# Eight short rows of unread matmuls behind the k steps of one phase of a tuned DFT and expert-mixture kernel

## The chip, the cores and the metric

The kernel runs on one core of a Trainium2 chip. The metric is the device time of one execution in microseconds (us). The engines are TensorE (PE, with its weight loads as PEld), VectorE (DVE), ScalarE (ACT), GpSimd (POOL) and SyncE (SP), which issues most DMAs.

## The reference

The output mixes two branches of one input x of 2048 tokens by 512 features, with a gate per token. Branch A is a two-sided DFT, of which the real part is kept. Branch B is a sum over 8 experts with softmax gates.

```python
a = einsum("bsd,ed->bse", x, dft_hid_re);  b = einsum("bsd,ed->bse", x, dft_hid_im)
A = einsum("ts,bse->bte", dft_seq_re, a) - einsum("ts,bse->bte", dft_seq_im, b)
B = sum_e softmax(xf @ w_gate)_e * (silu(xf @ w1[e]) @ w2[e])
out = g * A + (1 - g) * B          # g = sigmoid((x * gate_w).sum(-1))
```

## The kernel before

All large products are made of fp32r matmuls in three parts. A matrix is split into a high and a low piece, and the helper `mm` (lines 348 to 353) issues high x high (L349), high x low (L352) and low x high (L353) into one accumulator in PSUM. An accumulator is one bank, 128 partitions x 512 fp32; the pool `psp` has all 8 banks. A matmul takes 128 x 128 weights and 128 rows x 512 columns of the moving operand. Matmuls without a split, in plain fp32, occur at two places: ten in the warm-up (`warm`, L603, 128 x 128 columns) and the logits (L387), where each group of four puts its 32 columns of weights on a column tile of the array of its own.

The sequence DFT comes first. It has eight phases, by half of the output, by group of columns and by kind (X or Y). Each phase loops over NK = 8 values of k; for one k, a phase X issues the products 1, 2 and 5, each for two halves n, which is 18 matmuls into six banks, and a phase Y issues 6, 3, 7 and 4 into eight. The change concerns the phase (pr, c, ph) = (1, 1, "X"), the last phase X. Its predecessor is (1, 0, "Y") and its successor (1, 1, "Y"). For each k, `plan_right` loads a piece of the DFT matrix (SP), forms sums and splits it (DVE, ACT, once POOL); `plan_out_x` and `plan_out_y` read the finished banks (ACT and DVE) and store them. Behind the DFT come the second product of branch A and the experts, whose order is found by the planner `Plan`.

What sets the order: every operation is put on a list with a planned time (`ev`), the list is sorted, and the functions are called in that order. Compute instructions that are pinned (`pin`) keep this order on their engine; DMAs are not pinned, and the framework places them on SP's queue. It also assigns the banks of the pool and inserts the waits.

Of the kernel before, what the change touches and what calls it, by code (L numbers as in the profile page):

```python
# [8 lines left out]
F32 = mybir.dt.float32  # L9
# [7 lines left out]
P = 128  # L17
# [3 lines left out]
GT = 512  # L21
# [275 lines left out]
def fnet_moe_kernel(ctx: ExitStack, tc: tile.TileContext, x, xT, cT, wd, w1d, w2d, wg, out):  # L297


    nc = tc.nc  # L300
# [7 lines left out]
    psp = ctx.enter_context(tc.tile_pool(name="psp", bufs=8, space=PSUM))  # L308
    dram = ctx.enter_context(tc.tile_pool(name="dram", bufs=1, space=DRAM))

    def f32(ap_):
        return ap_.bitcast(F32)

    def sl(i):
        return slice(i * P, (i + 1) * P)
# [16 lines left out]
    def ev(t, fn, *args):  # L332

        evs.append((base[0] + t, len(evs), fn, args))

    def pin(ins):
        tc.keep_in_program_order(ins)
# [10 lines left out]
    def mm(ps, lh, ll, rh, rl, start, stop, first):  # L348
        ins = nc.tensor.matmul(ps, lh, rh, start=start, stop=False, skip_group_check=True)  # L349
        if first:  # L350
            pin(ins)
        nc.tensor.matmul(ps, lh, rl, start=False, stop=False, skip_group_check=True)  # L352
        nc.tensor.matmul(ps, ll, rh, start=False, stop=stop, skip_group_check=True)  # L353
# [21 lines left out]
    def plan_logits(T, dt):  # L375

        v = {}

        def load(d, a):
            v[d, a] = stage.tile([P, 2, GT], F32, tag="stage", name=f"xr{d}_{a}")  # L380
            nc.sync.dma_start(v[d, a], xT[d, :, 2 * a * GT:2 * (a + 1) * GT].rearrange("p (g t) -> p g t", g=2))

        def dots(d):
            if d == 0:
                v["p"] = psp.tile([P, GT], F32, tag="p", name="lt")
            for g in range(NG):
                ins = nc.tensor.matmul(v["p"][g * SQ:(g + 1) * SQ, :], wgs[:, d, :], v[d, g // 2][:, g % 2, :],  # L387
                                       start=d == 0, stop=d == ND - 1, skip_group_check=True)
                if g == 0:
                    pin(ins)  # L390

        def turn():
            pin(nc.vector.transpose(lg, v["p"]))

        ev(T - 12, lambda: nc.sync.dma_start(wgs[:, :, :E1], wg))
        for d in range(ND):
            t = T + dt * (1, 3, 5, 6)[d] + 2.6
            for a in range(2):
                ev(t - 9 + a, load, d, a)
            ev(t, dots, d)  # L400
        ev(t + 2.4, turn)
# [34 lines left out]
    xl, five, xraw = {}, {}, {}  # L436
# [8 lines left out]
    def plan_left_x(k, s, s5=None):  # L445

        v = {}
        s5 = s if s5 is None else s5

        def load(a, b):  # L450
            if a == 0:
                xraw[k] = xp.tile([P, 4, 256], F32, tag="x", name=f"xr{k}")
            nc.sync.dma_start(xraw[k][:, a:b, :], x[k][:, a:b, :])

        def s1():
            v["q"] = tmp.tile([P, 256], F32, tag="c", name=f"xq{k}_0")
            vt(v["q"], xraw[k][:, 2, :], xraw[k][:, 3, :], add)

        def hi():
            if k % 2 == 0:  # L460
                five[0] = xp.tile([P, 2, 2, 256], F32R, tag="x", name=f"xl5_{k}")
            v["w"] = five[0]
            act(v["w"][:, 0, k % 2, :], v["q"])
            xl[5, k] = (v["w"], k % 2)

        if s5 == s:
            ev(s - 14.5, load, 0, 4)
        else:
            ev(s - (14.5 if k else 31.5), load, 0, 2)
            ev(s5 - 14.5, load, 2, 4)  # L470
        left_pair(s - 4.7, s - 4.0, 1, 2, k, lambda: xraw[k][:, 0:2, :])
        ev(s5 - 3.3, s1)
        ev(s5 - 2.4, hi)
        ev(s5 - (0.9 if k == 1 else 0.5),
           lambda: vt(v["w"][:, 1, k % 2, :], v["q"], f32(v["w"][:, 0, k % 2, :]), sub))

    def plan_left_y(k, s, dt=None):

        v = {}

        def s3():
            v["q"] = tmp.tile([P, 2, 256], F32, tag="c", name=f"xq{k}_1")
            vt(v["q"][:, 0, :], xraw[k][:, 0, :], xraw[k][:, 2, :], sub)

        t = [s + dt * n for n in range(5)] if dt else [s, s + 0.5, s + 1.0, s + 2.0, s + 3.2]
        ev(t[0], s3)
        ev(t[1], lambda: vt(v["q"][:, 1, :], xraw[k][:, 3, :], v["q"][:, 0, :], sub))
        ev(t[2], lambda: vt(xraw[k][:, 1, :], xraw[k][:, 1, :], v["q"][:, 1, :], sub))
        left_pair(t[3] - 1.0, t[3], 7, 6, k, lambda: v["q"])
        left_pair(t[4] - 1.5, t[4], 3, 4, k, lambda: xraw[k][:, 1:4:2, :])  # L490
# [64 lines left out]
    def plan_right_0(k, s, s5, r):  # L555

        v = {}

        def load():
            v["a"] = stage.tile([P, 2, GT], F32, tag="stage", name=f"ca0{k}")  # L560
            if k:
                nc.sync.dma_start(v["a"], cT[0, 0, k][:, 0:2, :])
                return
            for j, queue in enumerate((nc.scalar, nc.sync)):
                queue.dma_start(v["a"][:, j, :], cT[0, 0, k][:, j, :])

        def load_d():
            v["d"] = tmp.tile([P, GT], F32, tag="c", name=f"cd0{k}")
            nc.sync.dma_start(v["d"], cT[0, 0, k][:, 2, :])

        def at(t_hi, t_lo, pool, tag, m, src):
            split_at(t_hi, t_lo, lambda: pool.tile([P, 2, GT], F32R, tag=tag, name=f"c0{k}_{m}"), src, vt,
                     lambda w: r.__setitem__(m, (w[:, 0, :], w[:, 1, :])))

        ev(s - (14.4 if k else 31), load)
        ev(s5 - 14.4, load_d)
        at(s - 4.0, s - 3.2, cp, "w", 1, lambda: v["a"][:, 0, :])
        at(s - 3.3, s - 2.6, cp, "w", 2, lambda: v["a"][:, 1, :])
        ev(s5 - 2.6, lambda: vt(v["d"], v["d"], v["a"][:, 0, :], sub))
        at(s5 - 1.8, s5 - (0.8 if k else 0.3), gp, "g", 5, lambda: v["d"])  # L580
# [24 lines left out]
    def dft(pr, c, k, ms, r, ps):  # L605
        for m in ms:
            w, j = xl[m, k]
            for n in range(2):
                if k == 0:
                    ps[m, n] = psp.tile([P, GT], F32, tag="p", name=f"u{pr}{c}_{m}{n}")  # L610
                mm(ps[m, n], w[:, 0, j, sl(n)], w[:, 1, j, sl(n)], *r[m], k == 0, k == NK - 1, True)

    def u_out(t, pr, c, i, j, n):
        nc.sync.dma_start(ud[c, 2 * pr + j, 2 * i + n], t[:, n, :])

# [100 lines left out]
    for pr, c, ph in phases:  # L716
        first = before is None
        dt = TY if ph == "Y" else TX0 if first else TXL if (pr, c) == (1, 0) else TX
        ps = {}
        for k in range(NK):  # L720
            s, r = T + k * dt, {}
            if first:
                if k < 2:
                    s, s5 = T + 2.72 * k, T + 5.44 + 1.36 * k
                    plan_left_x(k, s, s5)
                    plan_right_0(k, s, s5, r)
                    ev(s, dft_0, k, (1, 2), r, ps)
                    ev(s5, dft_0, k, (5,), r, ps)
                    continue
                plan_left_x(k, s)  # L730
                plan_right(pr, c, ph, k, s - 14, s - 2.9, r, lo=s - 3.4 if k == 2 else None)
            else:
                t = s - (6.8 if ph == "X" else 8.3)
                if before == "Y" and k == 1:
                    plan_right(pr, c, ph, k, t - 7, T - 4.0, r, pt, T - 2.1)
                else:
                    if before == "Y" and k == 2:
                        t = T + 3.4
                    plan_right(pr, c, ph, k, t - 7, t, r)
            ev(s, dft, pr, c, k, (1, 2, 5) if ph == "X" else (6, 3, 7, 4), r, ps)  # L740
        at = lambda k, o=0.0: T + k * dt + o
        if (pr, c, ph) == (0, 1, "X"):
            for k in range(NK - 3):
                plan_left_y(k, T + 6.2 * k + 0.4, 1.3)
        if (pr, c, ph) == (0, 0, "Y"):
            for k in range(NK - 3, NK):
                plan_left_y(k, T + 0.8 + (k - NK + 3) * 2.2 * TY, TY / 2)
        if (pr, c, ph) == (1, 0, "X"):
            plan_logits(T, dt)
        if (pr, c, ph) == (1, 0, "Y"):  # L750
            ev(at(2), softmax)
            ev(at(2, 4), softmax_end)
        if (pr, c, ph) == (1, 1, "X"):
            ev(at(2, 3.5), gate_rows)
            for n in range(4):
                plan_wd(n // 2, 2 * (n % 2), at(4 + n))
        if (pr, c, ph) == (1, 1, "Y"):
            for n in range(4):
                plan_uv0(n // 2, 2 * (n % 2), at(3 + n, 1))
        T += NK * dt  # L760
        if ph == "X":
            plan_out_x(pr, c, T, ps)
        else:
            plan_out_y(pr, c, T, ps, 14 if (pr, c) == (0, 0) else 7.5)
        before = ph
# [162 lines left out]
    for m in XORDER[:NX]:  # L928
# [4 lines left out]
        k = XORDER.index(m)  # L933
# [625 lines left out]
```

## Time and profile before

| | |
|---|---|
| median of 2 runs | 2020.7 us (2019.18 and 2022.22) |
| the profiled execution | 2019.07 us, its span 2017.3 us |
| PE busy | 2005.3 us, 99% of the span, 8836 matmul records |
| DVE, ACT, POOL busy | 82%, 51%, 42% |
| DMA | 475.19 MB, 236 GB/s on average |
| granted TensorE clock | 1.000 on average |

The span runs from the first to the last instruction. Busy shares are of the span. A matmul's record holds its whole passage through the engine, so neighbours overlap; the distance between two starts tells what one of them costs. An fp32 matmul is two records.

### The profile page before, as it was taken

Reading aid. Unit: us, or ns where it says so; the run is one execution under the profiler, and the core shown is the slowest. Engines: PE = TensorE matmul, PEld = TensorE weight load, DVE = VectorE, ACT = ScalarE, POOL = GpSimd, SP = SyncE. Lnnn points to the kernel's source line nnn. Section 1 sums busy time; section 2 is a strip of 40 time slices with the busy share of each in tenths; the row PEclk is TensorE's granted clock in tenths of the full one; section 3 lists DMA queues with packets and bytes.
Section 4 is the critical chain, followed back from the end, with each engine's and each line's share of the span. In section 5 each row is a group of like instructions: output and inputs, shape, how many; then the busy total and the mean of one; then the engine's idle time right before and its main releaser. Section 6 shows DMA issues by size and latency. Waiting matters only on the chain. (4 is left out here: it accounts for less than half of the span.)

```text
span 2017.3 us, 26775 instructions
## 1 busy us (share of the span) xinstructions
PE 2005.3 (99%) x8836; PEld 1651.1 (82%) x8836; DVE 1649.3 (82%) x1910; ACT 1020.9 (51%) x1427; POOL 848.9 (42%) x825
## 2 busy tenths in 40 slices
PE   9999999999999999999999999999999999999998
PEld 7887888888888888888878888888888888888887
DVE  8996996887878887887788787687778887899885
ACT  6543453455555555555555555544444444445442
POOL 0000000288889888889898820000002221233330
PEclk9999999999999999999999999999999999999999
DMA  8686686545565546454645599899889988999991
GB/s 316 215 269 215 237 306 218 187 149 179 173 202 172 188 159 213 165 194 164 222 156 176 177 307 377 296 338 288 266 264 289 289 269 257 285 282 323 315 284 42
DMA packets 204595, 475.19 MB, mean 236 GB/s; under 512 B 23172, under 2 KB 37892, under 8 KB 204456
## 3 DMA queue, kind: packets, MB, share of 16 engines
q1 hardware_dynamic: 191640, 450.15, 64.6%
q0 software_dynamic: 12672, 23.07, 6.8%
q8 instruction: 69, 1.13, 0.2%
q14 instruction: 70, 0.57, 0.1%
q10 hardware_dynamic: 144, 0.26, 0.1%
HBM read 366.36 MB, written 107.03 MB: 235 GB/s over the span
## 5 line engine op out<-in xcount | busy, mean ns | idle before, releaser
L1169 ACT ACTIVATE psp<-psp 128x512 f32<-128x512 f32 x280 | 160.3, 582 | 207.9 <-DVE psp L1153 141.3
L1153 DVE TENSOR_TENSOR psp<-psp,tc 128x512 f32<-128x512 f32 x79 | 55.3, 699 | 34.5 <-PE psp L353 28.1
L1068 POOL TENSOR_TENSOR tc<-ras 128x256 f32<-128x256 f32 x27 | 19.9, 738 | 137.2 <-DMA ras<-w_dram 135.9
L1231 ACT ACTIVATE tc<-psp 128x512 f32<-128x512 f32 x88 | 52.5, 597 | 43.6 <-PE psp L353 35.3
L1398 POOL DMA_DIRECT2D xfx1n<-w_dram x11 | 9.8, 978 | 128.1 <-DVE xf211n L1455 94.9
L1231 ACT ACTIVATE tg<-psp 128x512 f32<-128x512 f32 x67 | 40.0, 597 | 35.5 <-PE psp L353 26.3
L1153 DVE TENSOR_TENSOR psp<-psp,tg 128x512 f32<-128x512 f32 x52 | 36.3, 699 | 22.2 <-PE psp L353 16.8
L340 POOL TENSOR_TENSOR c73011l<-cb,c73011h 128x1024 fp32r<-128x1024 f32 x1 | 2.4, 2400 | 116.9 <-DMA ca<-cT_dram 116.9
L1083 POOL TENSOR_TENSOR wfs1nn<-tc,wfs1nn 128x512 fp32r<-128x512 f32 x32 | 41.9, 1311 | 15.6 <-ACT wfs1nn L1081 15.4
L1179 DVE TENSOR_TENSOR tc<-psp,tc 128x512 f32<-128x512 f32 x62 | 42.5, 685 | 5.3 <-ACT psp L1169 4.5
L1068 POOL TENSOR_TENSOR tc<-tc,ras 128x256 f32<-128x256 f32 x54 | 43.1, 798 | 4.2 <-DVE xfx13n L968 1.8
L1083 POOL TENSOR_TENSOR wfs3n<-tc,wfs3n 128x512 fp32r<-128x512 f32 x29 | 38.4, 1323 | 11.1 <-ACT wfs3n L1081 10.8
L1083 POOL TENSOR_TENSOR wfs2n<-tc,wfs2n 128x512 fp32r<-128x512 f32 x29 | 39.0, 1345 | 8.9 <-ACT wfs2n L1081 8.9
L1231 ACT ACTIVATE tw<-psp 128x512 f32<-128x512 f32 x41 | 24.5, 597 | 30.0 <-PE psp L353 24.6
L1083 POOL TENSOR_TENSOR wfs0n<-tc,wfs0n 128x512 fp32r<-128x512 f32 x26 | 35.3, 1356 | 7.8 <-ACT wfs0n L1081 7.6
L1153 DVE TENSOR_TENSOR psp<-psp,tw 128x512 f32<-128x512 f32 x37 | 25.9, 699 | 15.5 <-PE psp L353 13.5
L346 ACT ACTIVATE c<-cd 128x512 fp32r<-128x512 f32 x32 | 20.2, 631 | 33.0 <-DVE cd L343 32.6
L349 PE MATMUL psp<-xfx,wfs0n 128*128 128x512 f32 x94 | 36.7, 390 | 0.1
L353 PE MATMUL psp<-xfx,wfs0n 128*128 128x512 f32 x94 | 36.6, 389 | 0.0
L1083 POOL TENSOR_TENSOR wfs0n<-tg,wfs0n 128x512 fp32r<-128x512 f32 x24 | 32.2, 1340 | 7.7 <-ACT wfs0n L1081 7.7
L340 POOL TENSOR_TENSOR c12111l<-ca,c12111h 128x1024 fp32r<-128x1024 f32 x1 | 2.6, 2602 | 77.1 <-PE u L353 77.1
L1083 POOL TENSOR_TENSOR wfs3n<-tg,wfs3n 128x512 fp32r<-128x512 f32 x24 | 32.9, 1370 | 3.2 <-ACT wfs3n L1081 3.1
(3459 smaller groups left out, 7933.3 us busy)
## 6 DMA issues: line engine op xcount, KB each, us to landing
hd<-tc SPq DMA_DIRECT2D x161, 256.0 KB, 2.3
ca<-cT_dram SPq DMA_DIRECT2D x63, 512.0 KB, 5.6
hd<-tg SPq DMA_DIRECT2D x108, 256.0 KB, 2.4
hd<-tw SPq DMA_DIRECT2D x75, 256.0 KB, 2.4
cb<-cT_dram SPq DMA_DIRECT2D x32, 512.0 KB, 5.7
ras<-w_dram SPq DMA_DIRECT2D x29, 512.0 KB, 4.3
xfx12n<-hd SPq DMA_DIRECT2D x27, 512.0 KB, 5.8
ras1n<-hd SPq DMA_DIRECT2D x26, 512.0 KB, 4.8
```

The source lines that it names most:

```text
L340: pin(nc.gpsimd.tensor_tensor(*a))
L346: pin(nc.scalar.activation(dst, src, f, **kw))
L349: ins = nc.tensor.matmul(ps, lh, rh, start=start, stop=False, skip_group_check=True)
L353: nc.tensor.matmul(ps, ll, rh, start=False, stop=stop, skip_group_check=True)
L1068: pin(ins.tensor_tensor(low(b, j), src(x), src(y), o))
L1083: lambda: pin(nc.gpsimd.tensor_tensor(r(w)[:, 1, :], f(b), f(w)[:, 0, :], sub)), [oh] + deps, [b, w],
L1153: q = op("DVE", V, due, lambda: pin(nc.vector.tensor_tensor(f(dst), f(a[0]), f(b_[0]), o)), [a[1], b_[1]] + list(deps), [dst, a[0], b_[0]] ...
L1169: os = op("ACT", A, due, lambda: pin(nc.scalar.activation(f(dst), f(src_), AF.Silu, scale=sign)), [o0], [dst, src_])
L1179: oh = op("DVE", V, due + 1.2, lambda: pin(nc.vector.tensor_tensor(f(hb), f(dst), f(gb), OP.mult)), [os, og], [hb, dst, gb], lock=dst.ring ...
L1231: o = op("ACT", AP_, after(x), lambda: pin(nc.scalar.activation(f(b), f(bank[x[0]]), AF.Copy)), [prod[x]], [b, bank[x[0]]])
L1398: return op("POOL", 0.9, due, lambda: pin(nc.gpsimd.dma_start(f(src_)[:, j, :], block(key), accum_op=add, max_dma_last_dim=4096)), deps, [ ...
```

## The change

A new function `spare` is called behind the matmuls of each k in the phase (1, 1, "X"). It issues a row of matmuls on the operands of that k (the weight tiles w0 and w1 of product 1 and the moving piece m) into two banks of its own, `unread0` and `unread1`, which nothing reads. The output is computed as before. The rows differ from the plain stream in one thing each:

- k = 0: six matmuls of 256 columns, two weight tiles in turn
- k = 1: six with the same weight tile
- k = 2: six on the upper 64 rows of the array
- k = 3: six with 64 columns of weights
- k = 4: twelve, on the lower-numbered and the higher-numbered 64 rows in turn, on two banks
- k = 5: three in fp32 instead of fp32r
- k = 6: six that each open the sum anew
- k = 7: six on two banks in turn

```diff
+    unread = {}
+
+    def spare(k, r):
+
+        if k == 0:
+            for n in range(2):
+                unread[n] = psp.tile([P, GT], F32, tag="p", name=f"unread{n}")
+        a, b = unread[0], unread[1]
+        w, j = xl[1, k]
+        w0, w1 = w[:, 0, j, sl(0)], w[:, 0, j, sl(1)]
+        m = r[1][0]
+        half = slice(0, GT // 2)
+        low, high = slice(0, P // 2), slice(P // 2, P)
+        many = {
+            0: [(a[:, half], (w0, w1)[i % 2], m[:, half], False) for i in range(6)],
+            1: [(a, w0, m, False) for i in range(6)],
+            2: [(a, (w0, w1)[i % 2][low], m[low], False) for i in range(6)],
+            3: [(a[low], (w0, w1)[i % 2][:, low], m, False) for i in range(6)],
+            4: [((a, b)[i % 2], w0[(low, high)[i % 2]], m[(low, high)[i % 2]], False) for i in range(12)],
+            5: [(a, f32((w0, w1)[i % 2]), f32(m), False) for i in range(3)],
+            6: [(a, (w0, w1)[i % 2], m, True) for i in range(6)],
+            7: [((a, b)[i % 2], (w0, w1)[i % 2], m, False) for i in range(6)],
+        }[k]
+        for i, (ps, lhs, rhs, st_) in enumerate(many):
+            ins = nc.tensor.matmul(ps, lhs, rhs, start=st_ or i < (2 if k in (4, 7) else 1), stop=True,
+                                   skip_group_check=True)
+            if i == 0:
+                pin(ins)
...
             ev(s, dft, pr, c, k, (1, 2, 5) if ph == "X" else (6, 3, 7, 4), r, ps)
+            if (pr, c, ph) == (1, 1, "X"):
+                ev(s, spare, k, r)
```

On PE the rows stand between the plain matmuls of one k and those of the next. The first of them, in the piece of the difference below (u are the plain accumulators, xl the weights, c the moving pieces):

```order
 L352 MATMUL u_51_2132<-c_2064,xl_0_176 128x512
 L353 MATMUL u_51_2132<-c_2064,xl_0_176 128x512
+L637 MATMUL unread_2136<-c12110h,xl_12_115 128x256 x6
 L349 MATMUL u_10_2112<-c12111h,xl_12_130 128x512
 L352 MATMUL u_10_2112<-c12111l,xl_12_130 128x512
```

Six matmuls are new and the rows around them are the same. It is so at all eight places; on DVE, ACT and POOL no instruction moves.

On SP the queue changes at one place, near the end of the phase. Before (ca and cb are pieces of the DFT matrix for the next phase, tc<-xT_dram pieces of x for the experts, ud<-c finished results):

```order
L535 DMA ca_2332<-cT_dram 128x1024
L535 DMA cb_2334<-cT_dram 128x1024
L432 DMA tc_2792<-gTd 128x512
L535 DMA ca_2372<-cT_dram 128x1024
L535 DMA cb_2374<-cT_dram 128x1024
L903 DMA tc_2826<-xT_dram 128x512
L535 DMA ca_2454<-cT_dram 128x1024
```

And with the change:

```order
L535 DMA ca_2373<-cT_dram 128x1024
L535 DMA cb_2375<-cT_dram 128x1024
L432 DMA tc_2845<-gTd 128x512
L934 DMA tc_2879<-xT_dram 128x512
L934 DMA tc_2881<-xT_dram 128x512
L934 DMA tc_2900<-xT_dram 128x512
L535 DMA ca_2419<-cT_dram 128x1024
L535 DMA cb_2421<-cT_dram 128x1024
L934 DMA tc_2904<-xT_dram 128x512
```

Three loads of x now stand ahead of the next pair ca and cb; the fourth, which stood further back as well, comes right behind it.

## Rows read from the trace of the kernel before

**Rows 1.** The page: busy time of the engines, the granted clock in 40 slices of the span, and the chain that ended last, by engine and by line.
```profile
PE 2005.3 (99%) x8836; PEld 1651.1 (82%) x8836; DVE 1649.3 (82%) x1910; ACT 1020.9 (51%) x1427; POOL 848.9 (42%) x825
PEclk9999999999999999999999999999999999999999
PE 49%; DVE 0%; ACT 0%; issue 0%
PE psp L349 16%; PE psp L353 16%; PE psp L352 16%; DVE xfx9n L1360 0%; DVE xf31nn L1360 0%; ACT tw L1231 0%
```
**Rows 2.** Busy time by stretch: from:to, length, then PE, PEld, DVE, ACT and POOL busy (number of records), granted clock, DMA share, GB/s. The logits begin in the first stretch, the second is the changed phase, the third the phase behind it, and the last holds a stop of PE.
```profile
169.00:175.00 6.00, 6.00 (x30) 4.02 (x29) 5.52 (x7) 2.21 (x3) 0.00 (x0) 1.00 0.92 296
245.00:277.40 32.40, 32.40 (x144) 26.84 (x143) 30.14 (x42) 17.33 (x24) 0.00 (x0) 1.00 0.82 284
277.40:322.00 44.60, 44.60 (x198) 36.94 (x197) 39.98 (x48) 20.58 (x21) 0.00 (x0) 1.00 0.66 220
411.00:417.00 6.00, 4.97 (x22) 3.79 (x21) 4.61 (x5) 5.41 (x10) 3.56 (x4) 1.00 0.38 95
```
**Rows 3.** Instructions in order of time within the phase, PE and then its weight loads: start us, duration us, engine, line, operation, out<-in, array tile, shape.
```profile
270.62 0.39 PE L349 MATMUL u<-c12116h,xl 128*128 128x512 f32 x1
270.85 0.39 PE L352 MATMUL u<-c12116l,xl 128*128 128x512 f32 x1
...
272.66 0.39 PE L349 MATMUL u<-c,xl 128*128 128x512 f32 x1
...
270.62 0.19 PEld L352 LDWEIGHTS u<-c12116l,xl 128*128 128x128 f32 x1
270.85 0.19 PEld L353 LDWEIGHTS u<-c12116h,xl 128*128 128x128 f32 x1
```
**Rows 4.** The same view of PE around the first group of logits (lt), from overlapping short stretches: the last plain matmul, the first round of four records, the second round, and the first two plain matmuls behind.
```profile
170.39 0.39 PE L353 MATMUL u<-c,xl 128*128 128x512 f32 x1
170.70 0.64 PE L387 MATMUL lt<-xr,wgs 128*32 128x512 f32 x4
171.16 0.61 PE L387 MATMUL lt<-xr,wgs 128*32 128x512 f32 x4
171.70 0.50 PE L349 MATMUL u<-c12102h,xl 128*128 128x512 f32 x1
172.04 0.39 PE L352 MATMUL u<-c12102l,xl 128*128 128x512 f32 x1
```
**Rows 5.** The weight loads of the same place.
```profile
170.70 0.16 PEld L387 LDWEIGHTS lt<-xr,wgs 128*32 128x32 f32 x8 [0.35 <-DVE cd L343]
171.70 0.19 PEld L349 LDWEIGHTS u<-c12102h,xl 128*128 128x128 f32 x1 [0.84 <-ACT c L346]
171.81 0.19 PEld L352 LDWEIGHTS u<-c12102l,xl 128*128 128x128 f32 x1
```
**Rows 6.** The matmul records of all logits: duration of one in ns (least, median, most), first and last start in us.
```profile
L387 PE MATMUL lt<-xr,wgs x32: 592/604/617, 170.7 to 195.3; 128*32 128x512 f32 x32
```
**Rows 7.** The warm-up's fp32 matmuls: their loads (ns: least, median, most), and all records as one piece of the timeline (start, length in us).
```profile
L603 PEld LDWEIGHTS warm<-one x20: 288/333/337, 1.1 to 5.1; 128*128 128x128 f32 x20
...
1.14 4.61 PE L603 MATMUL warm<-one 128*128 128x128 f32 x20 [1.14 <-POOL one L600]
```
**Rows 8.** The timeline of DVE where it reads the last two sums of the phase before, and of PE at the last plain matmul of k = 0.
```profile
246.16 1.27 DVE L343 TENSOR_TENSOR c<-u,s 128x512 f32<-128x512 f32 x2
...
248.63 0.39 PE L353 MATMUL u<-c,xl 128*128 128x512 f32 x1
```
**Rows 9.** The timeline of ACT where it reads the first two sums of the changed phase, and of PE where the next phase begins.
```profile
274.22 1.28 ACT L346 ACTIVATE s<-u 128x512 f32<-128x512 f32 x2 [0.39 <-PE u L353]
...
277.42 0.39 PE L349 MATMUL u<-c64110h,xl 128*128 128x512 f32 x1
```
**Rows 10.** The timeline of SP's queue late in the phase.
```profile
268.05 0.42 SPq L432 DMA_DIRECT2D tc<-gTd  x1
272.32 0.33 SPq L535 DMA_DIRECT2D ca<-cT_dram  x1
```
**Rows 11.** All waits of PE from 320 us to the end: who waited for whom, us in total, times, longest.
```profile
PE psp L349 <- ACT tc L1231: 1.0, 1, 1.0
PE psp L353 <- POOL wfs2n L1083: 0.6, 1, 0.6
PE psp L349 <- ACT tw L1231: 0.2, 1, 0.2
```
**Rows 12.** The timeline of PE around its longest wait behind the DFT.
```profile
413.19 0.39 PE L353 MATMUL psp<-xfx,wfs0n 128*128 128x512 f32 x1
414.61 0.50 PE L349 MATMUL psp<-xfw,wfs2n 128*128 128x512 f32 x1 [1.03 <-ACT tc L1231]
```

## The prediction

> **What bounds the kernel now.** I read the page first. TensorE (PE) is busy for 2005.3 of 2017.3 us, the granted clock is full in every slice, and the chain that ended last is PE nearly throughout, split evenly over the three lines of the helper that issues a product [rows 1]. So the question is not who is late but how much PE time the change adds, and whether anything gives it back. The stretch of the changed phase comes next: from 245.0 us, just after it begins, to 277.4, where it ends, PE is busy for 32.40 of 32.40 us at clock 1.00, which is 2.4 GHz, and so it is in the phase behind [rows 2]. The other engines have gaps there. Then the single instructions. A plain matmul is listed with 0.39 us, but they overlap: nine starts, from 270.62 to 272.66, take 2.04 us, so the step is 0.2267 us, and that is the price of one more [rows 3]. Each has a weight load of its own, also where the weights are those of the matmul before (the first two lines of the helper); the load starts with the running matmul and lies under it [rows 3].
>
> **The change, part by part.** It removes nothing. It adds eight rows, one behind each k of this phase, 51 matmuls in all, in PE's own order; nothing reads what they write, so their whole time is on PE, and what counts is the step of each form.
>
> *k = 1, 6 and 7* (one weight tile six times; every matmul opening the sum anew; two banks in turn): plain size, 6 x 0.2267 = 1.36 us each, 4.08 together. The plain stream reloads equal weights already [rows 3]; it also changes bank every three matmuls and opens six sums at its first k, and the stretch shows no idle time [rows 2]. I see no reason for more or less.
>
> *k = 0* (256 columns): half a plain step is 0.113 us. The loads may become the limit: where PE resumes after a gap, two loads start 0.11 us apart (171.70 and 171.81) [rows 5]. So the floor is 6 x 0.11 = 0.66, the ceiling six plain steps, 1.36. Both rows that are near say just above 0.11; I take 0.12, 0.72 us.
>
> *k = 2 and 3* (64 rows of the array; 64 of its columns): the array is used as a smaller tile than in the plain stream. The only such place before is the logits, four fp32 matmuls on four column tiles of 32 [rows 4]. There the turn shows: the last plain matmul starts at 170.39 and would be through its step at 170.62, and the first tile starts at 170.70, 0.08 late. The second round of passes starts at 171.16, 0.46 after the first; 0.46 later is 171.62, but the plain matmul starts at 171.70, again 0.08 late, and its first step is 0.34 instead of 0.23, a bare load of 0.11 [rows 4, 5]. So a turn there and back is 0.08 + 0.08 + 0.11 = 0.27, and 0.11 more for the first load of 128 columns within the tile, 0.38; with 64 columns some 0.05 less. Inside the row I take plain steps: in the logits the loads of the second round were issued beside the first, eight within 0.16 us [rows 5], so tiles load ahead too. That makes 1.36 + 0.38 = 1.74 for k = 2 and 1.69 for k = 3. Without any turn each would be 1.36.
>
> The Trainium skill (TensorE: Matmul & The Clock Gate, "Part 3: Packing small matmuls — row/col tiling") says that a weight load overlaps matmuls in flight only when its row group differs. By that rule the six loads of k = 2 could not hide; the plain stream, always in the same row groups, hides every load [rows 3], so here the trace disagrees, at least for the whole array. For the half array no row decides, and it is a rival below.
>
> *k = 4* (twelve matmuls, upper and lower 64 rows in turn, on two banks): if two row tiles run side by side, this is six pairs, 6 x 0.2267 + 0.38 = 1.74; if they queue, 12 x 0.2267 + 0.38 = 3.10. The logits' four column tiles start together (four matmuls all within 0.64 us, where one is listed with 0.59 to 0.62) [rows 4, 6]; that is the nearest row, and I take 1.74.
>
> *k = 5* (three matmuls in fp32): an fp32 matmul is two records, and in the logits a record of 512 columns lasts 0.604 us [rows 6]. A plain one lasts 0.39 with a step of 0.23, so 0.16 is its tail; 0.604 less 0.16 is a step of 0.44, and six make 2.64 us. The floor is six plain steps, 1.36. The ceiling is from the warm-up, fp32 on the full array, 20 records of 128 columns in 4.61 us [rows 7]: some 0.22 each, and if that grew with the columns, four times it, 6 x 0.87 = 5.2. I take 2.64 since that row has the 512 columns; the warm-up's loads last 0.33 [rows 7] and can set its step by themselves. A turn of 0.38 between the types is possible; no row shows one, and I leave it to the range.
>
> *Waits.* The two new banks are those of the last two sums of the phase before; VectorE (DVE) has read them by 247.43 (246.16 + 1.27), and the first row begins behind the matmul of 248.63 [rows 8], 1.2 us of room. The next phase now begins in the bank of this phase's first sum instead of a free one. ScalarE has read the first two sums by 275.50, 1.9 us before the phase's end at 277.42 [rows 9], and the rows give it 1.36 us more. The tile that a row reads is held for one row longer, one or two us against a lead of several k: nothing. On SP's queue three loads of a quarter MB move ahead of a pair of DFT loads, 3 x 0.42 us of issue; the queue sits idle from 268.47 to 272.32 there [rows 10], so they fit in. Behind the phase PE is short of work for only 1.0 + 0.6 + 0.2 us [rows 11]: no more than that can be given back, and since the chain into those waits begins at PE itself, I take nothing.
>
> **Sum:** 0.72 + 1.36 + 1.74 + 1.69 + 1.74 + 2.64 + 1.36 + 1.36 = 12.6 us. The profiled execution took 2019.07 (1.8 outside its span), so its like will take 2031.7. The median of the two runs shown is 1.6 higher, which gives 2033.3; I say 2033.
>
> **The rivals.** *The row tiles queue.* k = 4 costs 3.10 instead of 1.74: about 2034.5. For it: no row shows two row tiles at once. Against it: the column tiles do overlap.
> *fp32 on the full array costs what the warm-up suggests*, or pays a turn: up to 2.6 more, about 2035.5.
> *Loads stay bare inside a half-array row.* Five more loads of 0.11 in k = 2 are 0.55: about 2033.5. This is the rule weighed above, and the plain stream speaks against it.
> *The end is given back.* If the 12.6 us let the other engines run ahead, the 1.8 us of later waits go: about 2031. It can't reach 2021, since 10.8 us remain.
> *The rows aren't executed* (the change does not do what it says): 2020.7. They stand in PE's program as written, so this is nearly excluded.
> *Slower by more than 2%* (40.4 us): the only mechanism that I find is the clock. If one of the odd rows made the granted clock fall to its lower level, 1.2 GHz, plain work would take twice its time; it decides from the point where 40.4 - 12.6 = 27.8 us of work, some 120 plain matmuls, run that way: about 2061. Against it: the clock stayed at 1.00 through the logits' tiles and through a stop of over one us at 413 [rows 2, 12], and each odd row is one to three us long with 4.1 us of plain stream around it.
>
> **How the numbers follow.** Forecast 65%, row tiles queue 15%, fp32 dearer 8%, bare loads 5%, given back 4%, the clock 2%, not executed 1%. The first five are all within 2% (what a measurement of this kernel tells from no change), so same is 97%, slower 2%, faster 1%. The range: downwards no turns (1.1 less) and some waits given back from the profiled 2031.7, 2029.5; upwards k = 4 queued and an fp32 row that is dearer, 2037. The runs shown spread over 3 us by themselves.
>
> **What will show it.** In the profile after: PE busy share unchanged and the span some 12.6 us longer; the distance between the two plain matmuls around each row, less one plain step, should be 0.72, 1.36, 1.74, 1.69, 1.74, 2.64, 1.36 and 1.36 us in the order of k. In k = 4 pairs of starts a few ns apart prove the overlap, equal distances of 0.23 refute it. Loads of k = 2 that start with the running matmul refute the bare ones. A fall of the granted clock anywhere between 245 and 325 us, or an idle PE where the next phase begins, would prove me wrong on what hides the rest.

## The result and the profile after

The changed kernel takes 2033.67 us (2033.49 and 2033.85), the ratio to the kernel before is put at 1.007 (the two medians alone give 1.0064), with a 95% interval of 1.0054 to 1.0087: slower, but by less than 2%. The profiled execution took 2033.49 us. The page of the kernel after, busy times and clock, as in [rows 1]:

```profile
PE 2017.7 (99%) x8890; PEld 1659.3 (82%) x8890; DVE 1644.9 (81%) x1910; ACT 1020.4 (50%) x1427; POOL 857.9 (42%) x825
PEclk9999999999999999999999999999999999999999
```

PE has 54 records and 12.4 us more (2017.7 - 2005.3), since the three fp32 matmuls are two records each; DVE, ACT and POOL have the same counts as before. The changed phase by stretch, as in [rows 2]:

```profile
245.00:291.00 46.00, 46.00 (x204) 35.79 (x203) 34.09 (x47) 19.17 (x28) 0.74 (x1) 1.00 0.73 240
```

PE is busy throughout at full clock; neither the new banks nor the moved loads make it wait. Now the rows, in the timeline of PE. For k = 0 to 5: the last plain matmul, the row as one piece, and the second plain matmul behind (start us, length us, line, names, array tile, shape, count):

```profile
249.68 0.39 PE L353 MATMUL u<-c,xl 128*128 128x512 f32 x1
249.90 0.88 PE L637 MATMUL unread<-c12110h,xl 128*128 128x256 f32 x6
...
250.85 0.40 PE L352 MATMUL u<-c12111l,xl 128*128 128x512 f32 x1
...
254.50 0.39 PE L353 MATMUL u<-c,xl 128*128 128x512 f32 x1
254.72 1.52 PE L637 MATMUL unread<-c12111h,xl 128*128 128x512 f32 x6
...
256.31 0.39 PE L352 MATMUL u<-c12112l,xl 128*128 128x512 f32 x1
...
259.94 0.39 PE L353 MATMUL u<-c,xl 128*128 128x512 f32 x1
260.25 1.66 PE L637 MATMUL unread<-c12112h,xl 64*128 64x512 f32 x6
261.84 0.50 PE L349 MATMUL u<-c12113h,xl 128*128 128x512 f32 x1
262.18 0.40 PE L352 MATMUL u<-c12113l,xl 128*128 128x512 f32 x1
...
265.82 0.39 PE L353 MATMUL u<-c,xl 128*128 128x512 f32 x1
266.05 1.54 PE L637 MATMUL unread<-c12113h,xl 128*64 128x512 f32 x6
...
267.66 0.39 PE L352 MATMUL u<-c12114l,xl 128*128 128x512 f32 x1
...
271.28 0.39 PE L353 MATMUL u<-c,xl 128*128 128x512 f32 x1
271.60 1.66 PE L637 MATMUL unread<-c12114h,xl 64*128 64x512 f32 x12
...
273.52 0.40 PE L352 MATMUL u<-c12115l,xl 128*128 128x512 f32 x1
...
277.17 0.39 PE L353 MATMUL u<-c,xl 128*128 128x512 f32 x1
277.40 2.74 PE L637 MATMUL unread<-c12115h,xl 128*128 128x512 f32 x6
...
280.20 0.39 PE L352 MATMUL u<-c12116l,xl 128*128 128x512 f32 x1
```

From the first to the last of each group are two plain steps and the row, so the row's cost is the distance less 0.453. For k = 1 that is 256.31 - 254.50 - 0.453 = 1.36. All eight:

| k | form | forecast | measured |
|---|---|---|---|
| 0 | 256 columns | 0.72 | 0.72 |
| 1 | same weights | 1.36 | 1.36 |
| 2 | 64 array rows | 1.74 | 1.79 |
| 3 | 64 weight columns | 1.69 | 1.39 |
| 4 | row tiles in turn, twelve | 1.74 | 1.79 |
| 5 | three fp32 | 2.64 | 2.58 |
| 6 | sum opened anew | 1.36 | 1.36 |
| 7 | two banks | 1.36 | 1.36 |
| | sum | 12.6 | 12.35 |

Two things are to be seen. In k = 2 and k = 4 the row starts 0.31 to 0.32 after the last plain matmul instead of 0.23, and the first plain matmul behind k = 2 needs 0.34 to the next (261.84 to 262.18): the turn. In k = 3 there is nothing of it, though the tile is listed as 128*64: 265.82 to 266.05 is one plain step. And twelve matmuls of k = 4 take as long as six of k = 2, so the two row tiles run side by side; record by record, they start in pairs 2 to 5 ns apart.

The weight loads of k = 2 and k = 4 in the same view (count at the end):

```profile
260.25 1.23 PEld L637 LDWEIGHTS unread<-c12112h,xl 64*128 64x128 f32 x6 [0.35 <-issue]
...
271.60 1.23 PEld L637 LDWEIGHTS unread<-c12114h,xl 64*128 64x128 f32 x12 [0.35 <-issue]
```

All six loads of k = 2 are over 1.23 us after the first began, before the last matmul starts at 261.52. Record by record, the first load stands bare (its matmul's step is 0.34), the second begins 0.11 behind it, and the other four begin with the row's second to fifth matmul: behind the first, the loads lie under the running matmuls.

The span grew by more than the rows: 2031.7 - 2017.3 = 14.4. Some of the rest was lost before the first row (the last plain matmul of its k starts at 249.68, before at 248.63 [rows 8]), so not to the change. PE's waits from 320 us on, beside [rows 11]:

```profile
PE psp L349 <- ACT tc L1262: 1.0, 1, 1.0
PE psp L349 <- ACT tg L1262: 0.9, 1, 0.9
PE psp L353 <- POOL wfs2n L1114: 0.6, 1, 0.6
PE psp L349 <- ACT tw L1262: 0.5, 1, 0.5
```

They sum to 3.0 instead of 1.8. Whether that is the change's doing was the first question for experiments; the second was why k = 3 pays no turn.

### The profile page after: what moved, and what is told of

It is laid out like the page before. It is cut to its first block, busy times and chain, and to the rows that moved or that the text cites. A ratio compares the mean times of both kernels' runs of the same rounds, so it can differ in the third digit from the quotient of the medians.

```text
span 2031.7 us, 26885 instructions
## 1 busy us (share of the span) xinstructions
PE 2017.7 (99%) x8890; PEld 1659.3 (82%) x8890; DVE 1644.9 (81%) x1910; ACT 1020.4 (50%) x1427; POOL 857.9 (42%) x825
```

## Experiments

All of them but the last change only what the function `spare` issues, or where; the output is computed as before. Row costs are read as above.

**One small matmul per row.**

```diff
-            0: [(a[:, half], (w0, w1)[i % 2], m[:, half], False) for i in range(6)],
...
+            0: [((a)[:, :32], w0, m[:, :32], True)],
+            1: [((b)[:, :32], w0, m[:, :32], True)],
...
```

> Each row is cut to one matmul of 32 columns; the two extra banks stay, and SP's queue stands as in the kernel before. Only row time counts (my theory): eight matmuls of at most 0.12 us, so 1 us or less more than before, about 2021.5; PE's waits outside the rows as scattered as between any two runs. Rival, the two extra banks or the place of the rows cost something by themselves: the 2 us that the span of the changed kernel grew beyond its rows (14.4 against 12.3) stay here, about 2023.5, with longer waits of PE than in the kernel before at the phase's ends or behind.

Measured: 2020.89 us against 2019.41, ratio 1.0007 (0.9998 to 1.0017). Each small matmul costs 0.12 to 0.13, 1.0 together; the span (2018.6) less that is 2017.6, beside 2017.3 before. The theory fits: in this execution the banks and the place cost no more than some tenths. The times alone do not decide, for their interval reaches to 3.4 us, and the rival asks for 3.0. The trace shows what a matmul of 32 columns is paid for; PE first, then its loads:

```profile
248.60 0.39 PE L353 MATMUL u<-c,xl 128*128 128x512 f32 x1
248.83 0.18 PE L637 MATMUL unread<-c12110h,xl 128*128 128x32 f32 x1
248.85 0.48 PE L349 MATMUL u<-c12111h,xl 128*128 128x512 f32 x1
249.18 0.40 PE L352 MATMUL u<-c12111l,xl 128*128 128x512 f32 x1
...
248.83 0.19 PEld L349 LDWEIGHTS u<-c12111h,xl 128*128 128x128 f32 x1
248.94 0.19 PEld L352 LDWEIGHTS u<-c12111l,xl 128*128 128x128 f32 x1
```

The plain matmul behind it starts 0.02 later, but its weights are then still being loaded, and its own step is 0.33 instead of 0.23. So the price is, but for about 0.01, the bare load of the next matmul: the two loads start 0.11 apart.

**Plain matmuls in all rows.**

```diff
-            0: [(a[:, half], (w0, w1)[i % 2], m[:, half], False) for i in range(6)],
...
+            0: [(a, (w0, w1)[i % 2], m, i == 0) for i in range(6)],
+            1: [(a, (w0, w1)[i % 2], m, i == 0) for i in range(6)],
...
+            7: [((a, b)[i % 2], (w0, w1)[i % 2], m, i < 2) for i in range(6)],
```

> All eight rows are six matmuls of plain size and type; SP's queue stands as in the changed kernel. Only row time counts: 8 x 1.36 = 10.9 us more than before, 2031.6, and 1.5 us less than the changed kernel's rows. Rival, the odd forms cost something behind themselves (in the clock or in the waits): PE's waits outside the rows fall back by the 2 us, about 2030 or less. Rival, the moved loads on SP's queue cost the 2 us: the waits stay as in the changed kernel, about 2033.

Measured: 2030.75 us against 2019.41, ratio 1.0055 (1.0038 to 1.0072). Each row costs 1.36, together 10.9, and 2019.41 + 10.9 = 2030.3 lies well inside the interval, which is 7.7 to 14.5 us above the kernel before and so holds the rivals too. The span less the rows is 2018.7, between the one before (2017.3) and the changed one (2019.4). So part of the surplus is there without odd forms; that they or the moved loads have no share in it is not shown by one trace of each kernel.

**Twice as many matmuls in every row.**

```diff
-            2: [(a, (w0, w1)[i % 2][low], m[low], False) for i in range(6)],
+            2: [(a, (w0, w1)[i % 2][low], m[low], i == 0) for i in range(12)],
...
```

> Every row has twice its matmuls (12, 12, 12, 12, 24, 6, 12, 12). One turn into and out of the half-array tile per row and plain steps inside (my theory): the rows take 1.44, 2.72, 3.17, 2.75, 3.18, 5.15, 2.72 and 2.72, together 23.9 us, about 2044.6. Rival, each matmul on the half array pays for itself: k = 2 and k = 4 double from 1.78 to 3.56. Rival, what came beyond the rows grows with the PE time that is added: the span grows by some 28 instead of 24, about 2048.

Measured: 2044.92 us against 2019.41, ratio 1.0125 (1.011 to 1.014), so 22 to 28 us more. The rows cost 1.44, 2.72, 3.17, 2.76, 3.17, 5.15, 2.72 and 2.72, together 23.9. k = 2 went from 1.79 to 3.17, not to 3.58: the turn is paid once per visit. The fp32 row doubled, 2.58 to 5.15. The span less the rows is 2019.3, so in the traces the surplus did not double with the time added; by the medians it is 25.5 - 23.9 = 1.6 us, give or take the three us of the interval.

**Column tiles and the type.**

```diff
+            0: [(a[q[0]], (w0, w1)[i % 2][:, q[0]], m, i == 0) for i in range(6)],
+            1: [(a[q[0]], f32((w0, w1)[i % 2][:, q[0]]), f32(m), i == 0) for i in range(3)],
+            2: [(a[low], f32((w0, w1)[i % 2][:, low]), f32(m), i == 0) for i in range(3)],
+            3: [(a[high], f32((w0, w1)[i % 2][:, high]), f32(m), i == 0) for i in range(3)],
+            4: [(b[(low, high)[i % 2]], f32(w0[:, (low, high)[i % 2]]), f32(m), i < 2) for i in range(6)],
+            5: [(a[q[i % 4]], f32(w0[:, q[i % 4]]), f32(m), True) for i in range(4)],
+            6: [(a[q[i % 4]], f32(w0[:, q[i % 4]]), f32(m), i < 4) for i in range(8)],
+            7: [(a, f32((w0, w1)[i % 2][low]), f32(m[low]), i == 0) for i in range(3)],
```

(q[i] are columns 32 i to 32 i + 31.)

> The rows become narrow-weight forms: k = 0 six fp32r with 32 columns of weights; k = 1 three fp32 with 32; k = 2 three fp32 with columns 0 to 63; k = 3 three fp32 with columns 64 to 127; k = 4 six fp32 on these two halves in turn; k = 5 the logits' form, four fp32 on four tiles of 32; k = 6 eight of them; k = 7 three fp32 on the upper 64 rows. Theory, fp32r with few columns is run as the whole array and only fp32 turns into a column tile: k = 0 takes 1.36 to 1.4 with no late start; k = 1 to 3 take six passes of 0.43 and a turn, 2.58 + 0.3 = 2.9 each; k = 4, halves side by side, also 2.9; k = 5 1.2 and k = 6 2.1 as 2 and 4 passes of 0.43 and a turn; k = 7 2.58 + 0.4 = 3.0. Rival, any column tile is free and the logits' turn came from four tiles at once or from the type: k = 2 and 3 take 2.58 like k = 5 of the changed kernel, and only k = 5 and 6 show late starts. Rival, halves queue: k = 4 takes 5.2 and a turn.

Measured in one execution of 2039.68 us: rows of 1.40, 2.90, 2.92, 2.92, 2.92, 1.20, 2.06 and 2.97 us. The timeline of PE at k = 0, 2 and 4, as above:

```profile
248.25 0.39 PE L353 MATMUL u<-c,xl 128*128 128x512 f32 x1
248.47 1.55 PE L638 MATMUL unread<-c12110h,xl 128*32 128x512 f32 x6
...
250.10 0.39 PE L352 MATMUL u<-c12111l,xl 128*128 128x512 f32 x1
...
260.74 0.39 PE L353 MATMUL u<-c,xl 128*128 128x512 f32 x1
261.05 2.79 PE L638 MATMUL unread<-c12112h,xl 128*64 128x512 f32 x6
263.77 0.50 PE L349 MATMUL u<-c12113h,xl 128*128 128x512 f32 x1
264.11 0.39 PE L352 MATMUL u<-c12113l,xl 128*128 128x512 f32 x1
...
274.82 0.39 PE L353 MATMUL u<-c,xl 128*128 128x512 f32 x1
275.13 2.80 PE L638 MATMUL unread<-c12114h,xl 128*64 128x512 f32 x12
...
278.19 0.39 PE L352 MATMUL u<-c12115l,xl 128*128 128x512 f32 x1
```

The theory holds on every row. With 32 columns in fp32r the row follows after a plain step (248.25 to 248.47) and costs 1.40; with 64 columns in fp32 it starts 0.31 behind the last plain matmul instead of 0.23, and the plain matmul behind pays its bare load (263.77 to 264.11). With few columns their number does not decide, the type does. Two halves in turn take twelve records in the time of six. A single tile turns as the logits' four do, so it wasn't their number either.

**Row tiles and short steps.**

```diff
+            0: [(b, (w0, w1)[i % 2][high], m[high], i == 0) for i in range(6)],
+            1: [(a, w0, m, i == 0) if i % 2 else (a, w1[low], m[low], i == 0) for i in range(6)],
+            2: [(a, (w0, w1)[i % 2][q[0]], m[q[0]], i == 0) for i in range(6)],
+            3: [(a, w0, m, i == 0) if i % 2 else (a[low], w1[:, low], m, i == 0) for i in range(6)],
+            4: [(a[low], (w0, w1)[i % 2][low, low], m[low], i == 0) for i in range(6)],
+            5: [(a[:, :P], f32((w0, w1)[i % 2]), f32(m[:, :P]), i == 0) for i in range(6)],
+            6: [(a[:, :P], (w0, w1)[i % 2], m[:, :P], i == 0) for i in range(12)],
+            7: [((a, b)[i % 2][:, :64], (w0, w1)[i % 2], m[:, :64], i < 2) for i in range(12)],
```

> The rows become: k = 0 six on the array rows 64 to 127; k = 1 three times one matmul on 64 rows and one plain; k = 2 six on 32 rows; k = 3 three times one with 64 columns of weights and one plain; k = 4 six on 64 rows with 64 columns; k = 5 three in fp32 with 128 columns of the moving operand; k = 6 twelve plain-type matmuls of 128 columns; k = 7 twelve of 64 columns. Theory, a visit to a row tile costs 0.09 late and 0.11 for a bare load each way, and the narrow fp32r weights are run as the whole array: k = 0, 2 and 4 take 1.79 like k = 2 of the changed kernel, k = 1 takes six plain steps and six one-way turns of 0.21, 2.6, and k = 3 1.39. The weight load sets the short steps: k = 6 and k = 7 take both 12 x 0.11 or just above, 1.35 to 1.5, and k = 5 six steps of 0.11 to 0.12 and at most 0.2 at its end, 0.7 to 0.9. Rival, the stream alone sets them: k = 6 0.8 to 0.9 and k = 7 0.5. Rival, the fp32 step of the warm-up (0.21 for 128 columns) holds here too: k = 5 1.3 or more. Rival, only a change of position or of both dimensions turns the array: k = 1 stays at 1.8 or k = 2 and 4 differ from k = 0.

Measured in one execution of 2034.74 us; k = 5 held six fp32 matmuls, twelve records, and not the three of the expectation. The rows: 1.78, 2.56, 1.79, 1.40, 1.74, 1.34, 1.35 and 1.35 us. Three of them in the timeline of PE:

```profile
255.71 0.39 PE L353 MATMUL u<-c,xl 128*128 128x512 f32 x1
256.02 2.63 PE L638 MATMUL unread<-c12111h,xl 64*128 64x512 f32 x6
...
258.72 0.39 PE L352 MATMUL u<-c12112l,xl 128*128 128x512 f32 x1
...
279.57 0.39 PE L353 MATMUL u<-c,xl 128*128 128x512 f32 x1
279.79 1.50 PE L638 MATMUL unread<-c12115h,xl 128*128 128x128 f32 x12
...
281.36 0.40 PE L352 MATMUL u<-c12116l,xl 128*128 128x512 f32 x1
...
290.48 0.39 PE L353 MATMUL u<-c,xl 128*128 128x512 f32 x1
290.71 1.42 PE L638 MATMUL unread<-c12117h,xl 128*128 128x64 f32 x12
...
292.28 0.40 PE L352 MATMUL u<-c64110l,xl 128*128 128x512 f32 x1
```

Half matmuls between whole ones (k = 1) cost 2.56, which is six plain steps and six one-way turns of (2.56 - 1.36) / 6 = 0.20. The same with narrow fp32r weights (k = 3) costs 1.40, no turn. The other half of the rows and a quarter of them (k = 0 and 2) behave like k = 2 of the changed kernel. A tile of 64 rows and 64 columns (k = 4) costs 0.05 less, all of it at the first step inside, 0.285 instead of 0.335: where a tile is turned to, a bare load of half the columns is that much shorter. Twelve steps are 1.34 to 1.35 us, 0.112 to 0.113 each, whether the matmul has 128 or 64 columns and also for fp32 records of 128: the weight load is the floor. The rivals fall, the one of the warm-up too: 0.11 per fp32 record here, 0.22 there [rows 7]; why it is twice as much there stands at the end.

**A row where PE waits anyway.** Beside the changed kernel:

```diff
-            if (pr, c, ph) == (1, 1, "X"):
+            if (pr, c, ph, k) == (1, 0, "X", NK - 1):
                 ev(s, spare, k, r)
...
+        for i in range(12):
+            ins = nc.tensor.matmul(a, (w0, w1)[i % 2], m, start=i == 0, stop=True, skip_group_check=True)
```

> The rows of the changed phase are gone; instead one row of twelve plain matmuls (2.72 us) stands at the end of the phase (1, 0, X), 0.3 to 3 us ahead of the only place in the DFT's middle where PE waits: from 202.5 to 205.5 us of the kernel before it loses 1.2 us to DVE, which is itself held up by a DMA. Theory, the rows of the changed kernel cost their full time because nothing was idle behind them: here the waits vanish from the trace and the span grows by some 1.5 us. Rival, DVE's reads follow PE, so that the waits move along and stay: the span grows by 2.7 us and the gaps are there, 2.7 us later.

Measured: 2021.62 us against 2019.94, ratio 1.0008 (0.9999 to 1.0017). Busy time by stretch at this place, first of the kernel before:

```profile
199.00:207.00 8.00, 7.61 (x32) 5.34 (x31) 6.05 (x8) 3.09 (x4) 0.00 (x0) 1.00 0.84 330
```

and with the row:

```profile
199.00:207.00 8.00, 8.00 (x37) 6.48 (x36) 5.16 (x7) 3.10 (x4) 0.00 (x0) 1.00 0.88 344
```

The gaps are gone: from 200 to 215 us the starts of PE's matmuls carry 0.08 us beyond plain steps, 1.26 before, and 1.1 to 2.3 in the seven other traces, where nothing was changed ahead of this place. 2.72 us of matmuls cost 1.7 by the medians; by the interval anything between nothing and 3.4, so it is the trace that decides for the theory.

**The change once more.**

> The changed kernel unaltered, timed beside the kernel before on one chip, since its span grew 14.4 us where its rows take 12.35. Theory, the other 2 us are scatter of PE's waits in the start, at 202 us and among the experts: the median difference lies at 12.4 to 13.4 with 12.4 inside the interval, and the profile shows other sizes of these waits than the first one did. Rival, the change lengthens later waits by 1 us or more: the difference is 14 or more and 12.4 lies outside the interval.

Measured: 2032.55 us against 2019.56, ratio 1.0066 (1.0052 to 1.008), a difference of 13.0 with an interval of 10.5 to 16.2. The rows cost the same 12.35 to the hundredth, and the span (2030.1) less the rows is 2017.8, against 2019.4 in the first profile and 2017.3 in the kernel before. The theory holds for most of the surplus: two executions of one program differ by 1.6 us outside the rows, in PE's waits. By the medians 13.0 - 12.35 = 0.7 us are left. The interval leaves room for anything from 2 us given back to 4 us lost, so that the change costs nothing beyond its rows is not shown to better than that by the times.

## Why the prediction was right

- **What bounds the kernel.** Right. PE was without a gap where the rows stand, and their 12.35 us are on the path in full. The row before a wait shows the other side: there part of the added time disappears.
- **Plain-sized rows (k = 1, 6, 7) and 256 columns (k = 0).** Right to 0.01 us.
- **k = 2 and k = 4, the turn.** The mechanism was right, the size 0.05 short: 0.43 instead of 0.38. The late start is 0.09 each way rather than 0.08, and the steps inside are 0.23 to 0.24, a little over the plain one.
- **k = 3.** The one wrong step: the turn of 0.33 itself. I took it from the logits, which differ in the type as well as in the tile, and put it down to the tile. The row cost 1.39 instead of 1.69, near the 1.36 that the prediction names for no turn at all. With fp32 in place of fp32r and the same 64 columns the turn appears. (That 64 columns make a turn some 0.05 cheaper is right where there is one: the tile of 64 rows and 64 columns.) The Trainium skill (TensorEngine Tiling (Array Packing), "Key Properties") says that changing the tiling mode drains TensorE. The row tiles and the fp32 column tiles fit that (0.09 late each way), though no run here shows what the lateness consists of; the fp32r rows listed as 128*64 and 128*32 start on time, so a narrow tile in the listing need not be a change of mode.
- **Row tiles side by side.** Right; the rival that they queue would have made k = 4 3.10.
- **Bare loads in a half array.** Refuted by the loads of k = 2 behind the first. The rule of the Trainium skill (TensorE: Matmul & The Clock Gate, Part 3), that loads hide only under another row group, does not hold inside any row here: they hide under the same group, on the whole array and on half of it. Only the first load behind a turn stands bare.
- **fp32.** 0.43 per record, taken as 0.44. The ceiling from the warm-up was no real one: the page's clock is full in every slice, but the warm-up ran at the lower level (last section), so its row was no price for this phase. No turn between the types is seen on the whole array.
- **Nothing given back, nothing lost.** Right within scatter: later waits were 1.8 us before and 3.0 after, but 2.3 in the repeat, with other sizes of the single waits, and 2.4 in the run with only 1.0 us of rows. So they don't grow in step with the added time (3.2 with the doubled rows). But 1.8 is the least of all nine traces, and whether the only trace of the kernel before is merely a low one stays open. The clock rival fell at once, 1.00 throughout the phase.
- **The total.** The sum was 0.25 too high: k = 3 was 0.30 over and fp32 0.06, the two turns 0.05 under each, so that part of the errors cancelled. The base, a median of two runs, was about 1 us above the medians that came later (2019.4 to 2019.9); the first two runs of the changed kernel were 1 us above its later median too. That 2033 met 2033.67 so closely is luck to that extent; 2032.55 is the better mark.

## What to carry to other kernels

On an engine that never waits, added instructions cost their steps, and these runs show nothing beyond them that is clear of the scatter; read the step from the distance of starts and count turns separately, once per visit. Before a price is carried over from the only row that shows an effect, list all that differs there: the logits differed in tile and type, and it took both to explain k = 3. Keep half-array matmuls together, for in turn with whole ones each pays 0.20 us, and pair them on the two halves, where the second six are free.

## What the runs showed beyond that

- An fp32r matmul with 32 or 64 columns of weights costs a plain step and no turn (1.40 and 1.39 for six); the same in fp32 pays 0.3. Why the type decides isn't shown by the runs.
- Cutting columns helps down to the weight load: 0.227 us for 512 columns, 0.12 for 256, 0.11 for 128 and for 64.
- The warm-up's fp32 records are twice as slow as the same form in the middle of the kernel, 0.22 against 0.11, though the view by stretch gives clock 1.00 there. Three runs show why (the column tiles, the row tiles and the row before a wait). The warm-up of the last of them, and its loads:

```profile
1.14 4.02 PE L603 MATMUL warm<-one 128*128 128x128 f32 x20 [1.14 <-POOL one L600]
L603 PEld LDWEIGHTS warm<-one x20: 192/333/333, 1.1 to 4.8; 128*128 128x128 f32 x20
```

It is 0.6 us shorter than before [rows 7], and its least load takes 192 ns instead of 288. Record by record, its step is 0.21 us up to 4.3 us and 0.11 from 4.4 us on, and the trace's first entry of the granted clock, 1.00, stands at 4.35. The two other runs step down likewise, at 4.6 and 4.0 us, with their first entries at 4.59 and 3.99. In the kernel before the first entry is at 5.59, and the warm-up ends at 5.75. So the warm-up ran at the lower level, 1.2 GHz, until that entry; ahead of it the trace has none, and the view shows 1.00 there for want of a record.
- In the same three runs the lower clock also reached into the first plain matmuls, behind the warm-up and a stop of 1.8 to 2.2 us. In the run with the row before a wait:

```profile
7.50:11.00 3.50, 3.50 (x10) 2.76 (x9) 3.14 (x7) 1.67 (x4) 0.00 (x0) 0.54 1.03 384
```

The plain step there is 0.43 us instead of 0.23. In the kernel before the same stretch has clock 1.00 and 17 records instead of 10. The span of that run shows little of it, as PE waits for its first operands there anyway: its stop at 16 us (0.6 before) is gone, and the one at 22 us is 0.7 instead of 1.2.
